# Columns of the inner layer dealt to units so that each partition loads neighbouring rows of w_out

## The chip, the cores and the metric

The kernel runs on one core of one Trainium2 chip. A core has five engines with instruction streams of their own (PE or TensorE for matmuls, DVE or VectorE, ACT or ScalarE, POOL or GpSimd, SP or SyncE) and 16 DMA engines that move data between HBM and SBUF, the memory next to the engines; PE writes to PSUM, in banks of 512 floats on each of 128 partitions. The metric is device microseconds of one launch; smaller is better. The kernel before took 291.41 us (median of three runs, 290.83 to 291.78).

## What is computed

Linear attention for 8 batches with 8 heads each, 576 positions and 64 channels, then a two-layer network with a swish gate over 4608 tokens of 512 channels, with 2048 columns in the inner layer:

```python
q_s = exp(q - q.max(-1));  q_s /= q_s.sum(-1) + 1e-9      # over channels
k_s = exp(k - k.max(2));   k_s /= k_s.sum(2) + 1e-9       # over positions
kv = einsum('bhsd,bhse->bhde', k_s, v)
x = einsum('bhsd,bhde->bhse', q_s, kv)                    # (8, 8, 576, 64) -> (4608, 512)
h = x @ w_in                                              # (4608, 2048)
g = h * sigmoid(beta * h)
out = g @ w_out                                           # (4608, 512)
```

The order of the 2048 inner columns is free, as long as the columns of w_in, the entries of beta and the rows of w_out are taken in the same order: `out` is a sum over them.

## The kernel before

Everything is one stream of named steps for each engine. `ORDER`, a list written out in the source, gives the order of all steps and, behind an equals sign, the engine of those that may run on several; the steps are issued in that order, and each engine works off its own in turn.

Attention (per batch b): `ld q/k/v` load through SP; `qmax`, `qsub`, `qexp`, `qsum`, `qrcp`, `qnorm` make the softmax of q (DVE, POOL, ACT, DVE, DVE, POOL); `kmax`, `kred`, `ksmall`, `krep`, `ksub`, `kexp` that of k without its division; `vcast` turns v into bf16; `kv` multiplies on PE, `kvn` normalizes; `qtr` and `qtrev` transpose q; `x` multiplies on PE and `xev` writes x to the tile `xT`. `fill` steps are matmuls on PE at the start whose results nobody reads.

The network works on chunks of 512 tokens (nine of them, eight batches and one of tails) and on 16 units of 128 inner columns: unit n has chunk n // 16 and u = n % 16. `h n` (L861) makes 128 columns of h for 512 tokens into one of four PSUM banks, from columns 128u to 128u + 127 of `w_in_b`, in four matmuls, or in halves for the first four units; `th n` (ACT, L879) takes the tanh with `beta_c[:, u]` as scale, one beta for each partition; `g n` (DVE, L896) gates and frees the bank; `o n` (L927) adds the product with `w_out_b[:, u, :]` to the accumulators of the chunk. So in `h` a column of the inner layer is a partition, and `beta_c` and `w_out_b` must have for partition p and unit u what column p of unit u stands for: before, this is column 128u + p.

Weights arrive in 16 loads of 512 KB on SP (`ld w n half`, L302 to L315), alternating w_in and w_out: n = 0, 2, 4, 6 are the four blocks of 512 columns of w_in, n = 1, 3, 5, 7 the four blocks of 512 rows of w_out, each in two halves (two of the four k tiles of w_in; two of four units for w_out). They land as float32 in the staging tiles `wst` (four of them: block n + 4 waits until the casts of block n are done). `cast w` (L317 to L325, helper at L228 to L232) turns a half, 1024 elements on each partition, into bf16 in `w_in_b` or `w_out_b`, on POOL or ACT as `ORDER` says. The casts of block 0 are split, 128 columns of each k tile (256 elements) and the remaining 384 (768 elements). Those of w_in: block 0, one small and one large cast on each of POOL and ACT; w2 both halves on POOL; w4 and w6 one half on POOL and one on ACT. Of the eight of w_out, six run on POOL and two on ACT.

Every partition of a w_out load gets two rows, 128 rows of w_out apart: runs of 2 KB (512 floats). Rows of a w_in load are likewise 2 KB for each k tile.

beta is loaded as 16 rows of 128 (L348), transposed by one matmul with the identity (L342), and copied by ACT to `beta_c` (L346).

The steps of `ORDER` around the first casts, which the prediction follows:

```
cast_w0_0_1=act, ld_w1_1, cast_w0_0_0=pool, cast_w0_1_1=pool, cast_w0_1_0=act, ..., xev_0_0_0=act, ...,
qsub_1_0=pool, ..., cast_w2_1=pool, ..., cast_w2_0=pool, ..., h_6, ..., qsub_1_1=pool, cast_w1_0=pool, h_5,
qexp_1_0, qsum_1_0, qrcp_1_0, th_6, ..., cast_w1_1=pool, ..., qnorm_1_0=pool, ..., cast_w4_1=act, ...,
cast_w4_0=pool, ..., qnorm_1_1=pool, ..., cast_w3_0=pool, ..., cast_w6_1=pool, ..., ksub_1_0=pool,
cast_w6_0=act, ..., ksub_1_1=pool, ..., cast_w5_0=pool, ..., o_8
```

Of the kernel before, what the change touches and what calls it, by code (L numbers as in the profile page):

```python
# [9 lines left out]
F32 = mybir.dt.float32  # L10
# [106 lines left out]
def kernel(  # L117
# [11 lines left out]
    P = 128  # L129
# [7 lines left out]
    NJ = FF // P  # L137
# [13 lines left out]
    def op(name, fn, eng=None):  # L151
        assert name not in ops, name
        ops[name] = (fn, eng)
# [4 lines left out]
    def sbt(name, shape, dt):  # L158
        return sb.tile(shape, dt, name=name)

    ident_f = sbt("ident_f", [P, P], F32)
# [2 lines left out]
    minus = sbt("minus", [P, P], F32)  # L164
    warm = sbt("warm", [P, P], BF16)
    first = sbt("first", [P, 1], F32)
    beta_rows = sbt("beta_rows", [NJ, P], F32)
    beta_c = sbt("beta_c", [P, NJ], F32)
    w_in_b = sbt("w_in_b", [P, KT, FF], BF16)
    w_out_b = sbt("w_out_b", [P, NJ, DM], BF16)  # L170
    wst = [sbt(f"wst{i}", [P, 4, 512], F32) for i in range(4)]
# [27 lines left out]
    place = {}  # L199
# [4 lines left out]
    def take(*who):  # L204
        assert sum(last in done for last, _ in turns) >= len(who), who
        for w in who:
            n = next(n for n, (last, _) in enumerate(turns) if last in done)
            i = turns.pop(n)[1]
            place[w] = ring[i][:]
            turns.append((w, i))  # L210

    def made(what, *parts):
        done.update((what, p) for p in parts)

    def uses(what, *parts):
        for p in parts:
            assert (what, p) in done, (what, p)
# [7 lines left out]
    dve, act, pool, pe, sp = nc.vector, nc.scalar, nc.gpsimd, nc.tensor, nc.sync  # L225
    ENGINES = {"act": act, "dve": dve, "pool": pool}

    def cast(eng, dst, src):  # L228
        if eng is act:
            act.copy(dst, src)  # L230
        else:
            eng.tensor_copy(dst, src)  # L232
# [62 lines left out]

    W = [(w, blk) for blk in range(4) for w in ("i", "o")]
    w_in_v = w_in.rearrange("(kt p) f -> p kt f", p=P)
    w_out_v = w_out.rearrange("(j p) f -> p j f", p=P)  # L300

    def load_w(n, half):  # L302
        which, blk = W[n]
        if n > 3:
            which, blk = W[n - 4]
            if which == "i":
                uses("i", *[(4 * blk + u, half) for u in range(4)])
            else:
                uses("o", 2 * blk + half)
            which, blk = W[n]  # L310
        dst = wst[n % 4][:, 2 * half : 2 * half + 2, :]
        if which == "i":
            sp.dma_start(dst, w_in_v[:, 2 * half : 2 * half + 2, 512 * blk : 512 * blk + 512])
        else:
            sp.dma_start(dst, w_out_v[:, 4 * blk + 2 * half : 4 * blk + 2 * half + 2, :])  # L315

    def cast_w(n, half, eng, c0=0, c1=512):  # L317
        which, blk = W[n]
        s = wst[n % 4][:, 2 * half : 2 * half + 2, c0:c1]
        if which == "i":  # L320
            made("i", *[(4 * blk + c // P, half) for c in range(c0, c1, P)])
            cast(eng, w_in_b[:, 2 * half : 2 * half + 2, 512 * blk + c0 : 512 * blk + c1], s)
        else:
            made("o", 2 * blk + half)
            cast(eng, w_out_b[:, 4 * blk + 2 * half : 4 * blk + 2 * half + 2, :], s)  # L325

    for n in range(8):
        for half in range(2):
            op(f"ld w{n} {half}", lambda n=n, half=half: load_w(n, half))
            if n == 0:  # L330
                for c, (c0, c1) in enumerate(((0, P), (P, 512))):
                    op(
                        f"cast w{n} {half} {c}",
                        lambda e, n=n, half=half, c0=c0, c1=c1: cast_w(n, half, e, c0, c1),
                        "pool",
                    )
            else:
                op(f"cast w{n} {half}", lambda e, n=n, half=half: cast_w(n, half, e), "pool")

    def beta_tr():  # L340
        take("beta")
        pe.transpose(place["beta"][:, 0:NJ], beta_rows[:], ident_f[0:NJ, 0:NJ])  # L342

    def beta_ev():
        done.add("beta")
        act.copy(beta_c[:], place["beta"][:, 0:NJ])  # L346

    op("ld beta", lambda: sp.dma_start(beta_rows[:], beta.rearrange("(j p) -> j p", p=P)))  # L348
    op("beta tr", beta_tr)
    op("beta ev", beta_ev)  # L350


# [404 lines left out]
    for h in range(3):  # L757
        i0, i1 = 4 * h, min(4 * h + 4, NI)
        for J in range(2):
# [4 lines left out]
            for w, j, n in parts:  # L764
                p = dict(j=j, n=n, i0=i0, i1=i1)
# [5 lines left out]
            if not summed:  # L771
                p = dict(j=2 * J, n=2, i0=i0, i1=i1)
# [219 lines left out]
    with tc.manual_schedule():  # L992
        for name, _, e in plan:
            fn, eng = ops[name]
            eng = e or eng
# [31 lines left out]
```

## Time and profile before

| what | value |
|---|---|
| runs | 290.83, 291.41, 291.78 us |
| profiled execution | 289.91 us, its span 287.9 us, granted TensorE clock 0.999 |
| loads of w_in, issue to landing (8, median) | 10.4 us |
| loads of w_out, issue to landing (8, median) | 11.4 us |
| load of beta, issue to landing | 8.1 us |
| w_in casts of 1024 elements | POOL 4 at 1039 ns, ACT 2 at 1053 ns |
| w_out casts of 1024 elements | POOL 6 at 1038 ns, ACT 2 at 1044 ns |
| first and last start of a w_in cast | 16.8 and 36.1 us |
| first and last start of a w_out cast | 24.9 and 53.5 us |
| bytes moved by DMA | 36.71 MB read from HBM, 9.44 MB written |

The span runs from the first to the last instruction of the profiled execution; the time of that execution holds 2.0 us more. A line of the profile names the source line, the engine, the operation and the tiles (out<-in); the cast helper's lines L230 (ACT) and L232 (the others) serve many steps, which are told apart by their tiles. "Idle before" is time in which the engine stood still just before an instruction, with what ended it.

### The profile page before, as it was taken

The numbers are of one execution on the slowest core, as the hardware profiler recorded it, in microseconds if no ns is written. First come the engines' busy times: TensorE is split into PE (matmuls) and PEld (weight loads), VectorE is DVE, ScalarE is ACT, GpSimd is POOL, SyncE is SP. The second block draws the span as 40 slices with busy tenths as digits, with TensorE's granted clock in tenths as the row PEclk, the third lists the DMA queues.
The fourth block names the chain that finished last, engine by engine and source line by source line (L and its number), as shares of the span: only waits on it lengthen the run. The fifth ranks groups of instructions, "written<-read, shape, count | busy, mean of one in ns | idle before, by whom it ended". The sixth has DMA issues, their size and how long they took to land.

```text
span 287.9 us, 5187 instructions
## 1 busy us (share of the span) xinstructions
PE 277.1 (96%) x1969; PEld 128.6 (45%) x1969; DVE 202.1 (70%) x413; ACT 175.0 (61%) x302; POOL 127.8 (44%) x90
## 2 busy tenths in 40 slices
PE   7769999999999999999999999999999999999994
PEld 3346544444443544444445444444444444444542
DVE  3989968999897989799888748544664354536330
ACT  4888895995777677566876356436643354334422
POOL 5899895498298894366964520340020000000000
PEclk9999999999999999999999999999999999999999
DMA  7999999899984999950023840800026003000404
GB/s 266 375 395 387 385 389 390 316 344 200 263 244 161 196 338 384 279 163 6 0 79 124 198 159 1 228 2 0 2 61 169 0 0 148 1 0 0 148 0 146
DMA packets 36808, 50.01 MB, mean 174 GB/s; under 512 B 15648, under 2 KB 15920, under 8 KB 36784
## 3 DMA queue, kind: packets, MB, share of 16 engines
q1 hardware_dynamic: 36640, 49.56, 53.0%
q8 instruction: 15, 0.25, 0.3%
q10 hardware_dynamic: 144, 0.13, 0.1%
q14 instruction: 9, 0.07, 0.1%
HBM read 36.71 MB, written 9.44 MB: 160 GB/s over the span
## 4 chain that ended last, share of the span: by engine, by line
PE 74%; DVE 9%; DMA 7%; ACT 4%; POOL 2%; issue 2%; SPq 1%; ACTq 0%; DVEq 0%
PE acc L927 36%; PE hT L861 34%; DMA out_dram<-osb 6%; DVE g L896 2%; POOL kf L543 2%; DVE km L478 2%; ACT th L879 2%; DVE qm L374 1%; PE hT L617 1%; DMA qf<-in_q_dram 1%; ACT xT L230 1%; DVE qs L420 1%; PE hT L667 1%; SPq L273 1%; DVE kf L543 1%
## 5 line engine op out<-in xcount | busy, mean ns | idle before, releaser
L879 ACT ACTIVATE th<-hT,beta_c 128x512 bf16<-128x512 f32 (+1 forms) x148 | 95.2, 677 | 72.1 <-PE hT L861 53.5
L896 DVE SCALAR_TENSOR_TENSOR g<-th,hT 128x512 bf16<-128x512 bf16 x144 | 94.4, 678 | 58.8 <-ACT th L879 49.2
L927 PE MATMUL acc<-w_out_b,g 128*128 128x512 bf16 x560 | 133.8, 380 | 0.1
L861 PE MATMUL hT<-xT,w_in_b 128*128 128x512 bf16 (+1 forms) x528 | 119.2, 373 | 2.3 <-ACT xT L230 1.2
L861 PEld LDWEIGHTS <-w_in_b 128*128 128x128 bf16 x592 | 57.5, 98 | 69.1 <-issue 3.2
L927 PEld LDWEIGHTS <-g 128*128 128x128 bf16 x560 | 53.4, 98 | 63.8 <-issue 3.1
L435 POOL TENSOR_TENSOR qn<-eq,qz 128x1152 bf16<-128x1152 bf16 (+2 forms) x20 | 34.6, 1738 | 54.3 <-DVE qz L427 33.7
L543 POOL TENSOR_TENSOR kf<-kf,kmb 128x1152 f32<-128x1152 f32 (+1 forms) x15 | 38.0, 2541 | 13.0 <-issue 5.3
L390 POOL TENSOR_TENSOR qf<-qf,qm 128x1152 f32<-128x1152 f32 (+2 forms) x19 | 33.4, 1767 | 16.0 <-DVE qm L374 12.5
L374 DVE TENSOR_REDUCE qm<-qf 128x9 f32<-128x576 f32 (+3 forms) x35 | 23.3, 689 | 4.6 <-DMA qf<-in_q_dram 4.6
L420 DVE TENSOR_REDUCE qs<-eq 128x9 f32<-128x576 bf16 (+2 forms) x33 | 23.0, 705 | 3.0 <-ACT eq L397 3.0
L478 DVE TRANSPOSE_TENSOR_REDUCE km<-kf 128x18 f32<-128x576 f32 (+1 forms) x30 | 23.4, 797 | 0.0
L397 ACT ACTIVATE eq<-qf 128x576 bf16<-128x576 f32 (+2 forms) x33 | 21.2, 658 | 3.1 <-POOL qf L390 3.0
L230 ACT CAST xT<-hT 128x512 bf16<-128x512 f32 x18 | 12.3, 741 | 14.7 <-PE hT L667 14.7
L591 ACT ACTIVATE ek<-kf 128x576 bf16<-128x576 f32 x32 | 20.6, 685 | 0.3 <-POOL kf L543 0.2
L232 DVE COPY osb<-acc 128x512 f32<-128x512 f32 x18 | 11.9, 681 | 4.0 <-PE acc L927 3.9
L861 PE MATMUL hT<-xTt,w_in_b 128*128 128x512 bf16 x64 | 14.6, 379 | 0.0
L230 ACT COPY osb<-acc 128x512 f32<-128x512 f32 (+1 forms) x18 | 10.0, 576 | 7.2 <-PE acc L927 3.1
L363 PE MATMUL hT<-g,warm 128*128 128x512 bf16 x26 | 9.4, 517 | 1.5 <-POOL g L238 1.5
L232 POOL CAST va<-vf 128x1152 bf16<-128x1152 f32 x8 | 9.2, 1148 | 2.0 <-PE hT L617 2.0
L230 ACT CAST va<-vf 128x1152 bf16<-128x1152 f32 (+1 forms) x10 | 9.4, 961 | 0.5 <-DMA vf<-in_v_dram 0.5
L232 DVE CAST xT<-hT 128x512 bf16<-128x512 f32 x10 | 6.7, 727 | 4.1 <-PE hT L667 4.0
(64 smaller groups left out, 113.1 us busy)
## 6 DMA issues: line engine op xcount, KB each, us to landing
qf<-in_q_dram SPq DMA_DIRECT2D x16, 576.0 KB, 6.0
kf<-in_k_dram SPq DMA_DIRECT2D x16, 576.0 KB, 7.1
vf<-in_v_dram SPq DMA_DIRECT2D x16, 576.0 KB, 7.9
out_dram<-osb SPq DMA_DIRECT2D x35, 256.0 KB, 3.5
wst<-in_moe_w_in_dram SPq DMA_DIRECT2D x8, 512.0 KB, 10.4
wst<-in_moe_w_out_dram SPq DMA_DIRECT2D x8, 512.0 KB, 11.4
out_dram<-osb SPq DMA_DIRECT2D x1, 128.0 KB, 2.1
out_dram<-osb ACTq DMA_DIRECT2D x1, 128.0 KB, 2.2
```

What stands on the lines that cost most here:

```text
L230: act.copy(dst, src)
L232: eng.tensor_copy(dst, src)
L374: dve.tensor_reduce(qm[:, j : j + n, i0:i1], qf[b % 2][:, j : j + n, i0:i1], axis=AX.X, op=ALU.max, negate=negate,)
L390: eng.tensor_tensor(x, x, m, ALU.subtract)
L420: dve.tensor_reduce(qs[:, i0:i1, j : j + n, 0:1], eq[:, i0:i1, j : j + n, :], axis=AX.X, op=ALU.add)
L435: eng.tensor_tensor(qn[b % 2][:, i0:i1, j : j + n, :], eq[:, i0:i1, j : j + n, :], z, ALU.mult)
L478: dve.tensor_reduce(km[:, j : j + n].rearrange("p j i e -> p (j i e)"), kf[b % 2][:, j : j + n].rearrange("p j i (e c) -> p (j i e) c", c=32),
L543: eng.tensor_tensor(x, x, m, ALU.subtract)
L861: pe.matmul(w, w_in_b[:, kt, u * P : (u + 1) * P], x[:, kt, cols(h)], start=(kt == 0), stop=(kt == KT - 1),)
L879: act.activation(th[turn(n, h) % 3][:, c], bank(n, h), ACTF.Tanh, scale=beta_c[:, u : u + 1])
L896: dve.scalar_tensor_tensor(out=out, in0=of, scalar=1.0, in1=src, op0=ALU.add, op1=ALU.mult)
L927: pe.matmul(acc[t][:], g[n % NG][:, t * P : (t + 1) * P], w_out_b[:, u, :], start=(u == 0), stop=(u == NJ - 1),)
```

## The change

Unit u = 4n + i of block n (n from 0 to 3, i from 0 to 3) gets the columns 512n + 4p + i, with p from 0 to 127, where it had 128u + p. A partition then needs rows 512n + 4p to 512n + 4p + 3 of w_out for the four units of a block, which are neighbours in HBM: a load of half a block brings two neighbouring rows, one run of 4 KB, to each partition. The loads of w_in are as before; their casts read every fourth float and write runs of 128. beta is loaded as four rows of 512, transposed in four matmuls of 128 entries each that take every fourth, and the copy to `beta_c` puts them in the order of the units. The casts of w_out, the engines and the order of all steps stay. On PE three matmuls are added (the transposes of beta); on the other engines the instructions are as many as before.

```diff
-    beta_rows = sbt("beta_rows", [NJ, P], F32)
+    beta_rows = sbt("beta_rows", [4, 4 * P], F32)
...
-    w_out_v = w_out.rearrange("(j p) f -> p j f", p=P)
+    w_out_v = w_out.rearrange("(n p u) f -> n p u f", p=P, u=4)
...
-            sp.dma_start(dst, w_out_v[:, 4 * blk + 2 * half : 4 * blk + 2 * half + 2, :])
+            sp.dma_start(dst, w_out_v[blk, :, 2 * half : 2 * half + 2, :])
...
     def cast_w(n, half, eng, c0=0, c1=512):
         which, blk = W[n]
-        s = wst[n % 4][:, 2 * half : 2 * half + 2, c0:c1]
+        s = wst[n % 4][:, 2 * half : 2 * half + 2, :]
         if which == "i":
-            made("i", *[(4 * blk + c // P, half) for c in range(c0, c1, P)])
-            cast(eng, w_in_b[:, 2 * half : 2 * half + 2, 512 * blk + c0 : 512 * blk + c1], s)
+            us = range(c0 // P, c1 // P)
+            made("i", *[(4 * blk + u, half) for u in us])
+            s = s.rearrange("p k (c u) -> p k u c", u=4)[:, :, us.start : us.stop]
+            to = w_in_b[:, 2 * half : 2 * half + 2, 512 * blk + c0 : 512 * blk + c1]
+            cast(eng, to.rearrange("p k (u c) -> p k u c", c=P), s)
...
-        pe.transpose(place["beta"][:, 0:NJ], beta_rows[:], ident_f[0:NJ, 0:NJ])
+        for u in range(4):
+            rows = beta_rows[:].rearrange("n (p u) -> n u p", u=4)[:, u]
+            pe.transpose(place["beta"][:, 4 * u : 4 * u + 4], rows, ident_f[0:4, 0:4])
...
-        act.copy(beta_c[:], place["beta"][:, 0:NJ])
+        w = place["beta"][:, 0:NJ].rearrange("p (u n) -> p n u", n=4)
+        act.copy(beta_c[:].rearrange("p (n u) -> p n u", u=4), w)
...
-    op("ld beta", lambda: sp.dma_start(beta_rows[:], beta.rearrange("(j p) -> j p", p=P)))
+    op("ld beta", lambda: sp.dma_start(beta_rows[:], beta.rearrange("(n c) -> n c", n=4)))
```

## The prediction

> **What bounds the kernel now.** I read the page first, then the busy times by stretch, the chain of waits, the timelines of POOL and ACT where weights are cast, and the groups by shape. From the page:
>
> ```profile
> span 287.9 us, 5187 instructions
> PE 277.1 (96%) x1969; PEld 128.6 (45%) x1969; DVE 202.1 (70%) x413; ACT 175.0 (61%) x302; POOL 127.8 (44%) x90
> ```
>
> and the busy times by stretch (busy us and count of each engine, then clock, DMA share, GB/s):
>
> ```profile
> 15.00:20.00 5.00, 3.44 (x100) 2.26 (x101) 4.78 (x15) 4.54 (x9) 5.00 (x5) 1.00 1.05 399
> 20.00:25.00 5.00, 4.29 (x36) 3.17 (x35) 4.02 (x7) 3.98 (x10) 4.88 (x7) 1.00 1.05 386
> 25.00:43.00 18.00, 17.87 (x97) 8.50 (x96) 15.26 (x32) 15.81 (x25) 15.63 (x11) 1.00 1.05 387
> 43.00:70.00 27.00, 27.00 (x276) 12.49 (x275) 25.02 (x52) 21.22 (x35) 18.43 (x11) 1.00 0.92 330
> 100.00:200.00 100.00, 99.59 (x707) 44.70 (x706) 75.16 (x158) 60.56 (x98) 48.93 (x24) 1.00 0.47 143
> ```
>
> From 25 us on PE hardly pauses: 0.13 us of 18, none of 27, 0.41 of 100. So a microsecond that PE loses in the first 43 us is paid in full at the end, and one saved elsewhere buys little. All weight casts lie there, and POOL is without a gap from 15 to 20 us and nearly so to 25. The chain of waits says which engine decides (start, us, what):
>
> ```profile
> 18.92 0.73 ACT xT L230
> ...
> 19.69 1.05 PE hT L861 x8
> ...
> 35.95 0.46 DVE kmb L533
> ...
> 36.48 5.20 POOL kf L543 x2
> 41.68 0.99 POOL w_out_b L232
> ...
> 42.71 1.02 PE acc L927 x4
> ```
>
> PE's first `h` waits for ACT's xT eviction, and `o 8` at 42.71 for a w_out cast that stood behind two `ksub` on POOL. Two places where a late ACT or POOL reaches PE at once. The timelines (start, us, engine line; in brackets idle time before):
>
> ```profile
> 17.66 1.15 ACT L230 CAST w_in_b<-wst 128x768 bf16<-128x768 f32 x2
> 18.91 0.73 ACT L230 CAST xT<-acc 128x512 bf16<-128x512 f32 x1
> ```
>
> ```profile
> 20.84 2.02 POOL L232 CAST w_in_b<-wst 128x1024 bf16<-128x1024 f32 x2
> 22.83 2.12 POOL L390 TENSOR_TENSOR qf<-qf,qm 128x1152 f32<-128x1152 f32 x1
> 35.02 1.04 POOL L232 CAST w_in_b<-wst 128x1024 bf16<-128x1024 f32 x1
> 36.48 5.20 POOL L543 TENSOR_TENSOR kf<-kf,kmb 128x1152 f32<-128x1152 f32 x2 [0.41 <-DVE kmb L533]
> ```
>
> The w_in casts stand directly in front of what the chain runs through: 0.1 us of slack on ACT at 18.81, 0.4 us on POOL at 36.06.
>
> **The change, part by part.** *w_out loads.* Eight loads of 512 KB keep their place on SP; their runs go from 2 to 4 KB. In the trace's packet records 2048 B take 85 ns (median) and 1024 B take 47, so 4096 B should take 85 + 2 x 38 = 161 against 170 for two. Each of 16 DMA engines gets 64 such pairs over all eight loads: 64 x 9 ns = 0.6 us less in some 50 us in which the DMA share is 1.05. After 12 us PE waits for no DMA anywhere, so I put the gain at 0; at most it is 0.6. The issue on SP (552 ns each) can shorten; SP isn't on the chain there.
>
> *beta.* One load of 16 rows of 512 B becomes 4 rows of 2 KB; the transpose becomes four, each near the 202 ns that the one took; the copy of 165 ns reads and writes in steps. PE stood 0.54 us for this load at 11.5, amid fill matmuls whose results nobody reads, and DVE decides until 18.2. Cover: these fills. Without it, 0.6 us for PE. I take 0.
>
> *w_out casts.* Same shape, engine and place: 0.
>
> *w_in casts.* Ten instructions keep their engine and place, but the source now goes in steps of four floats (16 bytes) inside a run of 128, where it was contiguous; the destination stays in contiguous runs. No row of the trace reads SBUF in such steps, so the price is bounded. The rows, by shape (busy us, mean ns, idle time before them):
>
> ```profile
> L232 POOL CAST w_in_b<-wst 128x1024 bf16<-128x1024 f32 x4 | 4.1, 1039 | 0.0
> L232 POOL CAST w_in_b<-wst 128x256 bf16<-128x256 f32 x1 | 0.4, 399 | 0.0
> L435 POOL TENSOR_TENSOR qn<-eq,qz 128x512 bf16<-128x512 bf16 x4 | 4.1, 1046 | 0.5 <-ACT eq L397 0.4
> L230 ACT CAST xT<-hT 128x512 bf16<-128x512 f32 x18 | 12.3, 741 | 14.7 <-PE hT L667 14.7
> L230 ACT COPY osb<-acc 128x512 f32<-128x512 f32 x17 | 9.6, 588 | 6.1 <-PE acc L927 3.1 <-DMA out_dram<-osb 3.0
> ```
>
> POOL: a cast costs (1039-399)/768 = 0.83 ns an element. An instruction that reads a second operand for each element costs, from qn at 1152 (2128 ns) and 512, 1082/640 = 1.69. Lower end 0; upper end one more read for each element, +0.86 ns, that is +0.88 us per 1024 elements. ACT: xT, written in steps of two elements, costs 153 ns more than a plain copy of as many, 0.30 ns an element; the upper end is its own 0.84 ns doubled. I take the upper end for POOL, because an element that shares no neighbouring read is nearest to the row with one more read, and for ACT the strided row: +0.31 us per 1024. Ends: nothing at all, and +0.88 and +0.86.
>
> [...]
>
> *Down the path.* ACT: the two casts at 17.66 hold 1024 elements, +0.31, less the slack of 0.1: first `h` 0.2 late. POOL: casts of w0 (1024 elements) +0.88, less some 0.1 of idle time: `qsub` at 20.0 and the w2 casts begin 0.76 late and end at 22.86 + 0.76 + 1.76 = 25.4. PE reaches `h 6`, their first reader, at 21.55 + 24 matmuls x 0.108 = 24.14, +0.2: it stalls 1.0 and is 1.2 late. The next `qsub` (22.83) ends 2.5 late. Behind it on ACT stands `qexp 1 0` (25.18), then tanh 6; behind those DVE's qz for the next `qnorm`. POOL's 0.63 us of idle time before `qnorm` at 27.54 is therefore mostly not to be had, since what it waits for moves too: it starts 2.2 late. The w4 cast adds 0.88 (3.1); the 1.32 of idle time before 31.97 is kept (1.8); the w6 cast adds 0.88 (2.7), 0.41 is kept: `ksub` starts 2.2 late and `o 8` too, PE's earlier 1.2 being contained in it. On SP the load of w4 waits for the w0 casts (2.9 us already), with the loads of k1 behind it; the DMA engines have some 5 us of loads queued then (w1 and w2, issued up to 13.3 and 11 us to land), so a slip under 1 us starves nobody. After 43 us PE is the bound and keeps what it lost.
>
> Sum: 0 + 0 + 0 + 2.2. The profiled execution took 289.91 us (span 287.9, 2.0 around it) and would take 292.1. It is 1.5 below the median of the runs shown, 291.41; on that I forecast 293.6.
>
> **The rivals.** (1) *Steps are free to read.* POOL's idle time and ACT's 0.1 cover whatever is left: 291.4. For it: strided writes of 16 bytes by ACT (xTt, 305 ns for 128 elements) cost little. Against: xT's 741.
>
> (2) *Half the price* (half of POOL's upper end, +0.43 us per 1024, with ACT's as above). w0 and w2: 1.2 late, which the 1.3 us before `h 6` just hides; `qsub` 1.2 late moves `qexp` and qz by about 1.0; w4 +0.43, 1.32 partly gone, w6 +0.43, 0.41 kept: about 0.9, with 0.2 if the idle time does absorb. 292.2. [...]
>
> (3) *The longer runs pay* (the other side). Where DMA ends last: POOL's `ksub` of batch 2 stood 3.1 us for a load at 57.58, and PE loses 0.7 us between 70 and 100, where the chain goes through loads. If casts cost nothing and loads land 0.6 us earlier, PE gets those 0.6 and some 0.3 more by 100 us: 290.5. It decides only while POOL is less than 0.4 us late at 36 us. Against: no wait of PE's names a load there.
>
> (4) *More than a doubling*, by POOL and ACT both at or above the upper end: ACT 2.3 late at the w6 cast that `h 13` needs at 37.23, POOL 3 at 42.7, and SP's loads slip so far that later batches wait: 295.5. Against: nothing in the trace has a read that dear.
>
> **How the numbers follow.** Forecast 0.44, its own spread 292.6 to 294.6; (1) 0.21; (2) 0.23; (3) 0.06; (4) 0.06. About 0.3% (0.87 us) is what a measurement of this kernel tells from no change. Slower: forecast 0.43, (4) 0.06, half of (2) 0.11: 0.60. Faster: (3) 0.06. Same: 0.34. The range, 291.0 to 295.2, leaves out (3), most of (4) and the lower part of (1).
>
> **What would show it.** Groups by shape: POOL's w_in casts of 1024 near 1.9 us and ACT's near 1.36, w_out casts unchanged at 1.04. PE idle before `h 6` about 1 us, busy time from 15 to 43 us down by about 2, and unchanged after. The w_out loads landing slightly below 11.4 us. I am wrong if the w_in casts stay at 1.04, if they are longer and PE's first 43 us are not, or if the difference arises after 43 us.

## The result, and the profile after

The changed kernel takes 295.49 us (median of four runs, 294.44 to 295.99) against 291.6 for the kernel before: ratio 1.0133, 95% interval 1.0098 to 1.0169. Repeated later beside further kernels it was 295.46 against 291.34, ratio 1.0146 (1.0112 to 1.0181). It is 4 us slower where 2.2 were forecast. (Ratios are taken over undisturbed runs alone and can differ from the quotient of two medians, for e2 below by 0.3%.)

The page after, with the row of the granted clock in 40 slices:

```profile
span 292.5 us, 5193 instructions
...
PE 279.2 (95%) x1972; PEld 129.8 (44%) x1972; DVE 202.1 (69%) x413; ACT 178.0 (61%) x302; POOL 132.7 (45%) x90
...
PEclk9797999999999999999999999999999999999999
```

Before, every slice had a 9. Here two have a 7. The busy times by stretch:

```profile
15.00:20.00 5.00, 4.29 (x106) 2.55 (x105) 4.78 (x16) 4.89 (x8) 4.89 (x6) 0.99 1.06 392
20.00:25.00 5.00, 3.13 (x20) 2.15 (x18) 3.29 (x7) 3.24 (x7) 5.00 (x5) 0.69 1.03 381
25.00:43.00 18.00, 17.02 (x98) 8.56 (x97) 14.86 (x32) 15.81 (x24) 17.81 (x11) 0.99 1.04 395
43.00:70.00 27.00, 27.00 (x200) 12.21 (x199) 23.01 (x48) 23.52 (x38) 18.67 (x11) 1.00 0.80 292
70.00:100.00 30.00, 27.94 (x213) 12.64 (x212) 25.47 (x57) 20.22 (x37) 22.08 (x11) 1.00 0.66 195
100.00:200.00 100.00, 100.00 (x794) 45.34 (x793) 79.54 (x169) 61.36 (x102) 52.46 (x25) 1.00 0.53 155
```

From 20 to 25 us PE is busy for 3.13 us where it was 4.29, and at a mean clock of 0.69; from 25 to 43 it is busy 0.85 us less than before. From 43 to 70 us and from 100 to 200 PE is full. From 70 to 100 us it stands still for 2.06 us, where before it was 0.70:

```profile
70.00:100.00 30.00, 29.30 (x227) 13.31 (x226) 26.77 (x63) 21.80 (x39) 22.50 (x12) 1.00 0.81 207
```

The casts by shape (busy us, mean ns, idle before):

```profile
L232 POOL CAST w_in_b<-wst 128x1024 bf16<-128x1024 f32 x4 | 8.1, 2028 | 0.0
L232 POOL CAST w_out_b<-wst 128x1024 bf16<-128x1024 f32 x6 | 6.2, 1038 | 0.0
L230 ACT CAST w_in_b<-wst 128x1024 bf16<-128x1024 f32 x2 | 4.1, 2062 | 0.0
L232 POOL CAST w_in_b<-wst 128x256 bf16<-128x256 f32 x1 | 0.6, 649 | 0.0
```

The w_in casts of 1024 elements take twice as long on both engines (2028 ns on POOL where it was 1039, 2062 on ACT where it was 1053): 1.80 ns an element on POOL ((2028-649)/768), where it was 0.83. The w_out casts have not moved (1038 ns on POOL before and after). The chain of waits now goes through ACT's casts and no longer through POOL's `ksub`:

```profile
18.59 1.17 ACT w_in_b L230
...
19.94 0.67 ACT w_in_b L230
20.61 0.64 ACT xT L230
...
33.57 1.94 ACT w_in_b L230
...
35.55 3.21 PE hT L868 x14
...
39.48 1.98 ACT w_in_b L230
...
41.50 3.63 PE hT L868 x16
```

Three times PE's `h` starts when an ACT cast is done: by way of xT at 21.29, directly at 35.55 and at 41.50.

Where the 4.6 us between the two profiled spans (287.9 and 292.5) arise is read off PE's timeline at three marks: first x matmul at 18.27 before and 19.09 after (+0.8), kv of batch 1 at 43.66 and 47.65 (a further +3.2), the end (+0.6; a wait near 95 us that was 0.7 is 2.1). The first 0.8 us lie ahead of any matmul that reads w_in: the chain of waits runs there through PE, which works at half the clock (0.50) from 11.67 to 15.08 us, and through beta's four transposes.

### The profile page after: what moved, and what is told of

Same layout as the page of the kernel before. It is cut to its first block, busy times and chain, and to the rows that moved or that the text cites. A ratio compares the mean times of both kernels' runs of the same rounds, so it can differ in the third digit from the quotient of the medians.

```text
span 292.5 us, 5193 instructions
## 1 busy us (share of the span) xinstructions
PE 279.2 (95%) x1972; PEld 129.8 (44%) x1972; DVE 202.1 (69%) x413; ACT 178.0 (61%) x302; POOL 132.7 (45%) x90
## 4 chain that ended last, share of the span: by engine, by line
PE 85%; ACT 6%; DMA 4%; DVE 2%; issue 1%; SPq 1%; POOL 1%; ACTq 0%
PE hT L868 40%; PE acc L934 39%; DMA out_dram<-osb 3%; ACT w_in_b L230 2%; PE hT L624 2%; DMA qf<-in_q_dram 1%; PE hT L674 1%; ACT xT L230 1%; DVE qm L381 1%; ACT th L886 1%; ACT ek L598 1%; SPq L273 1%; POOL qf L397 1%; PE hT L926 1%; PE acc L926 1%
## 5 line engine op out<-in xcount | busy, mean ns | idle before, releaser
L868 PE MATMUL hT<-xT,w_in_b 128*128 128x512 bf16 (+1 forms) x528 | 120.6, 376 | 4.9 <-DVE g L903 2.1
L232 POOL CAST w_in_b<-wst 128x1024 bf16<-128x1024 f32 (+2 forms) x6 | 10.2, 1720 | 0.0
```

Source lines behind the costliest of these rows:

```text
L868: pe.matmul(w, w_in_b[:, kt, u * P : (u + 1) * P], x[:, kt, cols(h)], start=(kt == 0), stop=(kt == KT - 1),)
```

## The experiments

Two theories stood at the start. A: all of the loss is the longer casts, and what they make PE wait. B: part of it comes from elsewhere in the change or from where the clock's windows fall. The stretch from the first x matmul to kv of batch 1, in which PE first reads what each w_in cast wrote, is the measure of the casts: 25.39 us before, 28.56 after. What the clock does in that time is contained in it.

**The parts of the change.** Plain casts on top of the change (e1), the steps alone on top of the kernel before (e2), steps on one engine alone (e3, e4):

```diff
 e1, e3, e4 (to the changed kernel; e3 shown)
-            s = s.rearrange("p k (c u) -> p k u c", u=4)[:, :, us.start : us.stop]
...
-            cast(eng, to.rearrange("p k (u c) -> p k u c", c=P), s)
+            if eng is pool:
+                s = s.rearrange("p k (c u) -> p k u c", u=4)[:, :, us.start : us.stop]
+                cast(eng, to.rearrange("p k (u c) -> p k u c", c=P), s)
+            else:
+                cast(eng, to, s[:, :, c0:c1])
```

> The changed kernel with w_in casts that read contiguously again (so w_in's columns are not in the order of beta and w_out's rows); the 4 KB loads of w_out and the new way of beta stay. Theory A (all of the loss comes from the longer casts, the half-speed clock windows at 11.8 and 22 us included, because PE starves): back to the kernel before, within 0.3% (290.7 to 292.4), granted clock 0.999, casts of 1024 at 1.04 us. Theory B (the first half-speed window comes from elsewhere in the change, beta's way or where the clock's windows fall): 0.8 to 1.6 us above the kernel before with a granted clock near 0.993.

> The kernel before with nothing changed but the w_in casts, which read every fourth float (so beta and w_out are not in that order). Theory A: all of the loss, +3.5 to +4.5 us, casts of 1024 at 2.03 to 2.06 us, granted clock 0.987. Theory B: +2.3 to +3.1 us, the first half-speed window missing, granted clock near 0.993.

> The changed kernel with only POOL's six w_in casts reading in steps, ACT's four contiguous (outputs not the reference's). If POOL's lateness decides, as forecast: +2 to +2.7 us over the kernel before. If ACT's casts decide, whose price I put too low (the chain after the change goes through ACT's casts at 18.5, 33.4 and 39.4 us, not through POOL): +0.5 to +1.5 us.

> The changed kernel with only ACT's four w_in casts reading in steps, POOL's six contiguous (outputs not the reference's). If POOL's lateness decides: +0.5 to +1.2 us over the kernel before. If ACT's casts decide: +2.5 to +3.9 us, with waits of PE for ACT's w_in casts of about 0.9 us in all and a half-speed window after the wait for xT near 20 us.

| kernel | median us (before beside it: 291.04) | ratio, 95% interval | mean clock of its runs | stretch x to kv |
|---|---|---|---|---|
| e1, 4 KB runs and beta's new way, plain casts | 291.03 | 0.9987 (0.9950 to 1.0023) | 0.992 (before 0.9935) | 25.43 |
| e2, steps alone | 295.15 | 1.0109 (1.0041 to 1.0176) | 0.9885 | 27.60 |
| e3, steps on POOL alone | 293.04 | 1.0077 (1.0038 to 1.0117) | 0.994 | 27.75 |
| e4, steps on ACT alone | 294.51 | 1.0115 (1.0053 to 1.0178) | 0.9865 | 29.20 |

So the casts carry the loss, as far as these intervals of 1 to 2 us either way tell: e1 is not told apart from the kernel before, nor e2 from the changed kernel. The 4 KB runs are worth nothing that can be measured. Their loads land 11.5 us after issue in the profile of e1 (median; a run of 294.44 us, the slowest of e1) and 11.1 in that of e8, which has 4 KB runs too, against 11.4 before. The 9.2 of the changed kernel can't be put down to the longer run: e2, steps with 2 KB runs, has 10.9, and no run separates the two. The medians make ACT's four casts dearer than POOL's six, and both together hardly dearer than ACT's alone, but the intervals of e3 and e4 overlap. In e3 PE's waits name POOL,

```profile
PE hT L871 <- POOL w_in_b L232: 2.0, 2, 1.5
```

in e4 they name ACT twice over (total us, times, longest):

```profile
PE hT L871 <- ACT xT L230: 2.2, 2, 1.5
...
PE hT L871 <- ACT w_in_b L230: 1.1, 2, 0.6
```

Beside that, the clock: e1's clock is that of the kernel before within the scatter of both (before ranged from 0.986 to 1.000 in 19 runs), so beta and the loads bring no half-speed windows that the kernel before doesn't have. Theory A had put e1 at 0.999, which the kernel before doesn't reach either (0.9935). But e2 and e4, like the changed kernel (0.986 to 0.988 in its first four runs), have a lower one.

**What a step costs** (e9), on the kernel before, and **what the loads need** (e8, e5).

```diff
 e9 (to the kernel before; durations alone)
+            step = {1: (2, 8)[half], 2: 2, 3: 8}.get(blk, 1)
+            if step > 1:
+                s = s.rearrange("p k (c u) -> p k u c", u=step)
+                to = to.rearrange("p k (u c) -> p k u c", u=step)
 e8 (to the changed kernel; beta and the loads of w_out in pairs likewise, the casts of block 0 split 512 and 512)
-    w_out_v = w_out.rearrange("(n p u) f -> n p u f", p=P, u=4)
+    w_out_v = w_out.rearrange("(n p u) f -> n p u f", p=P, u=2)
...
+            m = slice(us.start // 2, us.stop // 2)
+            s = s.rearrange("p k (m c u) -> p k m u c", m=2, u=2)[:, :, m]
+            cast(eng, to.rearrange("p k (m u c) -> p k m u c", c=P, u=2), s)
 e5 (to the changed kernel; casts plain)
-                w_in_b[:, kt, u * P : (u + 1) * P],
+                w_in_b[:, kt, 512 * (u // 4) : 512 * (u // 4) + 512].rearrange("p (c i) -> p i c", i=4)[:, u % 4],
```

> The kernel before with w_in casts of different steps, for their durations alone (columns of w_in are then in another order than beta and w_out's rows): w0 contiguous; w2 on POOL with steps of 2 floats (first half) and 8 floats (second half); w4, one half on POOL and one on ACT, steps of 2; w6, one on each, steps of 8. [...] If cost grows with the step: above 1.3 at 2 and well above 2.03 at 8. If every step costs the same: 2.03 at 2 too.

> Columns dealt in pairs (a unit takes every second column of 256), which is enough for 4 KB runs of w_out, since a load brings two rows to each partition; the casts then read in steps of two floats, 8 bytes. (The casts of block 0 are split 512 and 512 in place of 256 and 768.) If an engine pays for every step, or for an element that shares no 8 bytes: casts of 1024 near 2.03 us on both and +3 to +4 us over the kernel before. If two elements in 16 bytes are enough for the full rate: casts at 1.04 to 1.06 us and equal to the kernel before within 0.3%.

> The same dealing of columns and the same 4 KB loads of w_out as in the change, but the w_in casts read contiguously and PE's weight loads for h take every fourth column of w_in_b (bf16, 8 bytes apart). If the loss is the casts' price alone: equal to the kernel before (within 0.3%, 290.2 to 292.0), casts of 1024 at 1.04 us, PE's weight loads still near 98 ns. If steps cost PE as they cost POOL and ACT (doubled, 196 ns for 592 weight loads): they lie beside matmuls of 216 ns each, so between 0 and +10 us.

In e9 the casts of w4 and w6 on ACT and on POOL, first with steps of 2 floats and then of 8 (start, us):

```profile
30.60 1.14 ACT L230 CAST w_in_b<-wst 128x1024 bf16<-128x1024 f32 x1
...
36.08 2.06 ACT L230 CAST w_in_b<-wst 128x1024 bf16<-128x1024 f32 x1
```

```profile
29.95 1.11 POOL L232 CAST w_in_b<-wst 128x1024 bf16<-128x1024 f32 x1
...
34.96 2.04 POOL L232 CAST w_in_b<-wst 128x1024 bf16<-128x1024 f32 x1
```

| step in bytes | 4 | 8 | 16 | 32 |
|---|---|---|---|---|
| POOL, 1024 elements, us | 1.04 | 1.11 | 2.03 | 2.04 to 2.05 |
| ACT, 1024 elements, us | 1.05 | 1.14 | 2.06 | 2.06 |

The cost doesn't grow in proportion to the step; it jumps once, between 8 and 16 bytes, and on both engines alike (1.11 to 2.03 us on POOL, 1.14 to 2.06 on ACT). e8 keeps to 8 bytes, which the loads allow, as each brings only two rows to a partition: 291.28 us against 291.19, ratio 1.0010 (0.9973 to 1.0048). The loss is gone, as far as this interval tells. e5 leaves the step to PE's weight loads, bf16 elements 8 bytes apart: 114 ns where they took 98, beside matmuls of 216 (0.86 us for four in the chain before). That is no doubling. Its time is 292.05 us, ratio 1.0026 (0.9996 to 1.0057), which leaves open whether it is slower than the kernel before; and its stretch is 26.36 us, a microsecond longer. The trace shows another cause than the weight loads for most of that: POOL's second w2 cast waits 2.06 us for PE's `h` (idle time ahead of POOL's w_in casts of 1024 is 2.5 us in all, 0.0 before and after), and PE then waits 0.83 us for this cast.

**What the clock adds.** In the profile after the granted clock changes at 11.67, 15.08, 21.91 and 25.32 us, in steps of 3.41 us or twice that. The stretches of this grid, called windows here:

```profile
8.25:11.67 3.42, 1.64 (x9) 0.80 (x7) 3.28 (x6) 2.96 (x11) 3.03 (x5) 1.00 1.06 392
11.67:15.08 3.41, 3.41 (x15) 1.74 (x15) 2.72 (x8) 2.44 (x6) 2.40 (x3) 0.50 1.04 386
15.08:18.49 3.41, 3.09 (x90) 2.04 (x88) 3.34 (x9) 3.38 (x7) 3.30 (x5) 1.00 1.06 392
18.49:21.91 3.42, 1.77 (x26) 1.08 (x24) 2.15 (x9) 2.75 (x4) 3.42 (x3) 1.00 1.05 399
21.91:25.32 3.41, 2.80 (x15) 1.72 (x14) 2.82 (x5) 2.21 (x5) 3.41 (x4) 0.50 1.03 369
```

Of these five, each window in which PE was busy for less than 1.8 us (the first number behind the window's length; 1.64 and 1.77 us) is followed by one at half the clock (0.50). The first of them ends at 11.67 us, before a w_in cast has begun (17.59 us), so the casts can't have brought it. The second is the one with PE's wait of 1.26 us for xT behind ACT's casts. If that wait is the cause, filling PE's wait must raise the clock:

```diff
 e7 (to the changed kernel), e11 (to e4)
+    FILLS = ... + [(7, None)]                      # fill_17: seven matmuls
-x_0_1_1, x_0_1_0, qsum_0_2_0, ...
+x_0_1_1, x_0_1_0, fill_17, qsum_0_2_0, ...
 e12 and e15 (to the kernel before), e13 (to e8), e14 (to the changed kernel): besides, the first fill longer;
 fill_17 has three matmuls in e12, e13 and e15, seven in e14
-    FILLS = [(14, None)] + ...
+    FILLS = [(22, None)] + ...
```

> The changed kernel with seven fill matmuls (0.22 us each at the full clock) put on PE between the x matmuls and the first h, where PE waits 1.3 us for ACT's casts and xT. If that wait brings a window at half the clock (22 to 25.5 us in the profile after): granted clock up from 0.987 to near 0.993, one half-speed window less, and 0.8 to 1.7 us faster than the changed kernel (293.0 to 294.5 against 295.2). If the windows come at any rate: the same clock, and equal or up to 0.4 us slower.

> The changed kernel once more, unaltered, beside the next three. Theory (casts 2.0 to 2.3 us through 43 us, and about one half-speed clock window more than the kernel before, each 3.4 us long and so 1.7 us of matmul): +3.5 to +4.3 us, granted clock 0.985 to 0.990 against 0.994 to 0.996 before. If the low clock of the first runs was chance: +2.0 to +2.5 and the clock of the kernel before.

> The kernel with steps in ACT's casts alone, and seven fill matmuls on PE ahead of the first h, where PE waits 1.5 us for ACT. Theory: the clock comes up from 0.987 to about 0.995 and +3.5 us shrinks to what ACT's late casts cost alone, +1.7 to +2.3. If ACT's casts themselves cost 3.5 us: no change by the fills, +3.3 to +3.9.

> The kernel before with 22 instead of 14 matmuls in the first fill and three more ahead of the first h. If half-speed windows follow from gaps of PE in the first 20 us: clock 0.998 or more, 0.3 to 1.0 us faster than before. If PE's gaps at 90 us bring as many, or the fills delay the q transposes: within 0.3% of before.

> The columns dealt in pairs (4 KB runs, steps of 8 bytes) with the same two longer fills. Casts at 1.11 to 1.14 us, so 0.1 us late per cast; with the clock held as in the kernel before with fills: equal to that one within 0.3%, and not slower than the kernel before. If the 4 KB runs are worth anything to PE: 0.3 us or more faster than that one.

> The changed kernel with 22 matmuls in the first fill and seven ahead of the first h. With the clock held (0.997 or more) only the casts' lateness is left. Theory: +2.0 to +2.6 us over the kernel before with both fills (e15), that is near 291.3, within 0.3% of the kernel before. If the casts cost the whole 4 us by themselves: +3.5 to +4.2 over e15. If the clock is most of it: +0.5 to +1.5.

> The kernel before with 22 matmuls in the first fill and three ahead of the first h once more, as the yardstick of e14: 289.1 again (288.6 to 289.9), granted clock 0.998 or more, ratio near 0.991 to the kernel before.

| kernel | median us (before beside it) | ratio, 95% interval | mean clock (before) | stretch x to kv |
|---|---|---|---|---|
| e10, changed kernel again | 295.46 (291.34) | 1.0146 (1.0112 to 1.0181) | 0.986 (0.992) | 28.54 |
| e7, changed, 7 fills ahead of `h` | 292.93 (291.19) | 1.0048 (1.0020 to 1.0076) | 0.995 (0.995) | 28.17 |
| e11, steps on ACT alone, 7 fills | 292.47 (291.34) | 1.0026 (0.9997 to 1.0055) | 0.994 (0.992) | 27.53 |
| e14, changed, both fills | 292.77 (290.99) | 1.0048 (1.0021 to 1.0076) | 0.999 (0.994) | 28.21 |
| e12, kernel before, both fills | 289.08 (291.34) | 0.9913 (0.9885 to 0.9942) | 0.999 (0.992) | 25.50 |
| e15, the same again | 290.01 (290.99) | 0.9955 (0.9924 to 0.9985) | 0.998 (0.994) | 25.50 |
| e13, pairs, both fills | 289.67 (291.34) | 0.9947 (0.9919 to 0.9974) | 0.997 (0.992) | 25.57 |

In the profile of e7 the two windows around the wait:

```profile
17.02:20.43 3.41, 2.70 (x62) 1.49 (x61) 3.23 (x11) 3.41 (x6) 3.41 (x4) 1.00 1.06 398
20.43:23.84 3.41, 2.70 (x21) 1.76 (x19) 1.68 (x6) 2.11 (x5) 3.41 (x4) 1.00 1.01 385
```

Matmuls whose results nobody reads bring the changed kernel from +4.1 to +1.7 us, although the casts read in the same steps. The fills don't let `h` start earlier (2.39 us after the first x matmul in e7, 2.20 in the profile after), so these 2.4 us are not the wait itself; what does change with them is the clock (0.986 without the fills, 0.995 with them). With the wait filled, the changed kernel (e7, +1.7) is where steps on POOL alone are (e3, +2.0), and steps on ACT alone are at +1.1 (e11): most of what ACT's casts add goes away when that wait is filled.

How much of the 4.1 us is the casts' lateness and how much the clock is told less sharply. With the clock held in both, the difference is 292.77 - 290.01 = 2.8 us (e14 and e15; resampling the runs gives a 95% interval of 1.6 to 3.6), and the stretches differ by the same (28.21 and 25.50, 2.7). The yardstick itself moved: the same kernel took 289.08 in e12. In e2, whose profile has no half-speed window between 18 and 96 us, the stretch is 27.60, so the casts cost 2.2 to 2.8 us there. That the remaining 1.3 us are half-speed windows is not shown. One such window more is 3.41 / 2 of 292 us, or 0.0058 of the clock, and the changed kernel's clock is lower by 0.006 to 0.007: the count fits one. But within the stretch the window costs the changed kernel only 0.4 us (28.56 after, 28.21 and 28.17 in e14 and e7), where it costs steps on ACT alone 1.7 (29.20 in e4, 27.53 in e11). At the full clock PE waits instead for POOL's casts, a wait that the profile after doesn't have (e14):

```profile
PE hT L868 <- POOL w_in_b L232: 1.0, 2, 0.5
```

More is gained behind the stretch: the wait near 95 us (2.1 in the profile after, 2.6 in that of e10) is 1.3 in e7 and gone in e14, and from kv to the end the changed kernel takes 244.9 us in its profile and 243.1 in that of e14 (the kernel before 244.2, and 243.1 in e15). Whether the early windows set that wait was not tried.

The kernel before with both fills is faster than the kernel before, by 0.87% in one session and 0.45% in the other. e13 is faster than the kernel before too, and not told apart from e12; the gain of the 4 KB runs over e12 that one branch of its expectation named didn't come (289.67 and 289.08). Several expectations had the direction right and the size wrong: e7 and e12 gained more than was written down (2.5 us over the changed kernel where 0.8 to 1.7 was put, and 2.3 over the kernel before where 0.3 to 1.0 was), e11 lost less (+1.1, put at 1.7 to 2.3), e14 lost a little more over e15 (2.8, put at 2.0 to 2.6), and e15 itself came in at 290.01, above its 288.6 to 289.9.

## Why the prediction failed where it did

*PE bounds the kernel, and what it loses in the first 43 us is paid.* Right in the main: 4.0 of the 4.6 us between the spans exist at 47.65, and 100 to 200 us is as good as full in both. The busy time was to be unchanged after 43 us, though, and from 70 to 100 us it is 1.36 us less.

*w_out loads, beta, w_out casts at nothing.* Within the 1 us that e1 can tell, right. The packet records have 164 ns for 4096 B where 161 was estimated, and the w_out casts stayed at 1.04 us. For beta the cover was taken too lightly: the four transposes take 0.61 us where the one took 0.20, and in e1 and e4, which have them, beta's load stands in the chain of waits with 3% of the span, where before it ran through DVE (in e2, which has the one, the load stands in it too). PE waits 0.7 us for the load in e5 and 0.77 in e12, which has the one transpose of before; x starts at 18.91 in e5 and at 18.49 in e12. These 0.4 us are near the 0.6 that the text named and set aside; whether they reach the end is not shown.

*POOL's price, +0.88 us per 1024 elements.* The chosen end was the right one: +0.99. That it is a second read for each element, the reason given, was not tested.

*ACT's price, +0.31 us per 1024.* This step failed. I took ACT's strided write as the nearest row for a strided read; it measured +1.01, above the upper end of +0.86 that the text had written down and put aside. The first `h` was to come 0.2 late; it waited 1.26 us where it had waited 0.48, and 0.8 was lost there. The runs e3, e10 and e7 show what hangs on it, each against the kernel before beside it: with POOL's steps alone the time is +2.0 us, with ACT's added it is +4.1, and with PE's wait for ACT filled it is +1.7. The same mis-sizing hid a direct path: in the changed kernel `h 8` waits for ACT's w4 cast at 35.5 and `h 13` for its w6 cast at 41.5 (0.32 and 0.57 us), places at which the forecast looked at POOL.

*The path on POOL, 2.2 us late at the `ksub`.* For POOL alone it holds: e3 measured +2.0, 2.4 in the stretch, with PE's longest wait of 1.5 us before `h 6`, where 1.0 was put. In the changed kernel PE waits for no cast of POOL's, since ACT's lateness comes first; the casts together cost 2.2 to 2.8 us of the stretch at the full clock, where 2.2 was the sum. That the sum is at the lower end of this is partly luck, as it came from POOL's path alone.

*The clock.* The sum had no term for it, and this failed too. The row of the clock in the page before was 9 throughout, and I took it as given. It isn't: in these traces the clock granted to PE goes with how busy PE was one window of 3.41 us before (counted below), and a longer wait of PE's where it has gaps can cost a second time: with its wait of 1.26 us for xT, PE is busy for 1.77 us of the window from 18.49 to 21.91 in the profile after, and the next window has 0.50. The windows lie at another offset in each run (one begins at 7.44 us before, at 8.25 after). The gaps need not be as long as a window: PE's longest waits in e1, e2 and e10 are 2.3 to 2.6 us, and gaps that add up to 1.5 us of a window were enough in 13 cases of 14.

*The rivals.* Free steps and half the price are out by the durations. The longer runs that pay are out by e1 and e8. The time is that of the last rival (295.5), whose price, both engines at or above the upper end, is what was measured; but that the time agrees is in part luck: of the lateness that it expected (3 us at `o 8` and loads that slip) the casts gave 2.2 to 2.8, and the rest goes with PE's wait and its clock, which no rival had.

## What to carry to other kernels

Price a strided read by the bytes between its elements and not by the fact that it strides: for these float32 casts of 1024 elements 8 bytes were nearly free (1.11 us on POOL and 1.14 on ACT, against 1.04 and 1.05) and 16 doubled the time (2.03 and 2.06). So deal rows or columns only as far as the load needs (pairs gave the same 4 KB runs at no cost that could be measured, e8: ratio 1.0010), and ask first whether longer runs are on the path at all (here they were not, e1: ratio 0.9987). And where PE has gaps, look at a new wait twice, once as itself and once by the clock of the next window (0.50 in 13 cases of 14 here); a few matmuls without a purpose in the gap were a cheap cover (2.5 us off the changed kernel in e7).

## What the runs showed of the hardware

The cost of a cast from float32 to bf16 jumps between steps of 8 and 16 bytes and is flat from there up to 32: for 1024 elements 1.11, 2.03 and 2.04 to 2.05 us on POOL, 1.14, 2.06 and 2.06 on ACT (e9 and the profile after).

The clock: in all 16 profiles I set PE's busy time in each window of the clock's grid, in the first six windows at work and in five around 90 us, against the clock of the window behind it. Of 14 full-clock windows with PE busy for less than 1.9 of 3.41 us, 13 were followed by half the clock (0.50); of those above, one was (2.06 us). The one that was not followed by half is the changed kernel's own window at 93.59 us (1.76 us busy); why is open. The 1.9 was read off these same windows, and the border isn't sharp: three windows with 1.93 to 2.04 us busy (e14, e2, e5) were followed by the full clock. Most runs of the kernel before have a lower clock too, and the profile that the prediction was made from (0.999) happened to show no such window before 287 us: 13 of its 19 runs beside e1 to e4 have 0.994 or less, all 19 from 0.986 to 1.000, with times from 290.21 to 293.46. With the fills of e12 the mean is 0.999.

Not tried: what sets the wait of 0.4 to 2.6 us near 90 us, which differs from profile to profile, is missing in e11, e12 and e14, and in e1, e2 and e10 is followed by a half-speed window of its own.
